# Attention and a PReLU MLP on one core: score tiles in bursts of three, small inputs as rows, and a later second load

## The chip, the cores and the metric

The kernel runs on one core of a Trainium2 chip. Five engines work side by side, each through its own queue in order: TensorE (PE; its weight loads are shown as PEld), VectorE (DVE), ScalarE (ACT), GpSimd (POOL) and SyncE (SP), which only issues DMAs here. ACT and POOL issue DMAs too. The metric is the device time of one execution in microseconds (us), lower is better.

## The reference

Per head, q and k are normalised by their root mean square over the 64 elements of a head and scaled by g_q and g_k; then comes softmax attention, and a two-layer MLP with a parametric ReLU over all heads of a token. The shapes are 8 batches, 12 heads, 448 positions, head size 64, so 768 model columns, and 2048 MLP columns. In and out are float32.

```python
def rmsnorm(x, g):
    rms = np.sqrt(np.mean(x * x, axis=-1, keepdims=True) + 1e-06)
    return x / rms * g
q_n, k_n = (rmsnorm(q, g_q), rmsnorm(k, g_k))
scores = np.matmul(q_n, k_n.transpose(0, 1, 3, 2)) / np.sqrt(64)
attn = np.exp(scores - np.max(scores, axis=-1, keepdims=True))
attn = attn / (np.sum(attn, axis=-1, keepdims=True) + 1e-09)
x = np.matmul(attn, v).transpose(0, 2, 1, 3).reshape(3584, 768)
h = x @ w_in
out = (np.maximum(h, 0.0) + alpha * np.minimum(h, 0.0)) @ w_out
```

## The kernel before

The 96 heads are worked in 24 groups of four: a group y has batch y // 3. Everything is laid out by hand; a tile framework adds the semaphores, and the order on each engine is the order in which the program is written (`manual_schedule`).

**One group.** `load_qk` (L88) brings q and k, two DMAs each, by SP; of groups 0 and 1 ACT issues one half. `square` (L120) and `reduce` (L130) give the sums of squares: the square is on ACT for groups 0 and 1, on POOL later; the reduction is on VectorE. `root` (L138) is two activations on ACT, Ln and Exp. `scale` (L147) multiplies q or k by it and writes float16, on POOL (on VectorE for three early ones). `turn` (L157) transposes both with 14 TensorE matmuls into the PSUM tile tps, and VectorE copies it to qT and kT; kT is multiplied by the product of the gains on the way.

A group has seven score tiles. `score` (L184) makes one with four matmuls of shape 64*64, `soft` (L198) takes its exponential on ACT from PSUM to expT. There are two PSUM buffers for score tiles (pool pss). When the seven tiles are done, `den` (L221) sums them with 28 matmuls against ones (dn), `log` (L225) and `invert` (L230) turn the sum into its reciprocal by Ln and Exp on ACT, and `attv` (L234) multiplies expT with v in 28 matmuls (av); VectorE writes the product with the reciprocal to xT. The PSUM tiles tps, dn and av share one buffer (pool psa).

**The MLP of a batch.** `up` (L245) is one of 16 units: six matmuls (hT, shape 128*128), then ah = alpha * h on ACT, then gT = max(h, ah) on VectorE, in float16. `down` (L262) is one of 14 units for two batches: 16 matmuls (op), a copy to osb on VectorE, and after the second half two output DMAs on SP. Both use the two PSUM buffers of pool psf. Down units of a pair of batches are possible when their columns of gT are there.

**The order.** The 168 score tiles go two at a time; such a pair with what follows it is called a burst here (L413 to L457), 86 in all. The last two bursts hold no tiles. In a burst stand, in this order: the two score tiles; dn, if a group's last tile was in the burst before (`dens`); av one burst later (`avs`); the exponentials; log; roots; a turn, if one is due (`turns`); then the ups and downs that were dealt to this burst (`gaps`), and inversion after the second up or after all units. In bursts with neither dn, av nor turn whose first unit is an up, the second exponential is put behind that up (`wait`). The dealing (L348 to L370) spreads a batch's units over the bursts of the next batch's attention by estimated costs (`cost`, UP, DOWN). Units that are left are in `rest` and come after all bursts. Bursts before `first` have no units and get idle matmuls (`spin`, L284) instead, which keep TensorE running.

Loads and squares are placed by burst as well (`prep`, `post`, `jobs`, L306 to L326): group y's load eight bursts, its squares two bursts ahead of its reduction; reductions in `jobs` are issued inside the first down of the burst, ahead of its copy, or else at the burst's end. POOL's queue holds, besides squares and scalings, the DMAs of v, w_in and w_out.

**The start.** Group 0's loads, the table load on ACT (L381), the gains by POOL, one element per partition (L382 to L384), groups 1 and 2, and alpha by SP, transposed by the access pattern into 128 partitions (L387). Then come 34 idle matmuls on TensorE, the squares, roots, scalings and turn of group 0, and v and w_in on POOL.

Of the kernel before, what the change touches and what calls it, by code (L numbers as in the profile page):

```python
# [9 lines left out]
FP32 = mybir.dt.float32  # L10
# [11 lines left out]
def kernel(  # L22
# [12 lines left out]
    nc = tc.nc  # L35

    B, H, S, D = q.shape
    DM = H * D
    DF = moe_w_in.shape[1]
    J = S // 64  # L40
# [34 lines left out]
    idle = cst.tile([128, S], FP16, name="idle", tag="idle")  # L75
    nc.vector.memset(idle, 0.0)
    gain = cst.tile([128, 1], FP32, name="gain", tag="gain")
    gk2 = cst.tile([128, 1], FP32, name="gk2", tag="gk2")
    alpha_sb = cst.tile([128, NF], FP32, name="alpha_sb", tag="alpha_sb")
    w_in_sb = cst.tile([128, KM, DF], FP16, name="w_in_sb", tag="w_in_sb")  # L80
# [6 lines left out]

    def load_qk(y):  # L88
        b, i = divmod(y, G)
        for nm in "qk":  # L90
            t = ld.tile([128, 2, J, D], FP32, name="nat", tag="nat", bufs=6)
            for g in range(2):
                (nc.scalar if y < 2 and g else nc.sync).dma_start(
                    out=t[ds(64 * g, 64)].rearrange("p h j d -> p h (j d)"),
                    in_=SRC[nm][b, g, :, ds(2 * i, 2)],
                )
            nat[y, nm] = t
# [197 lines left out]

    NB = (NG * J + 1) // 2

    def last(y):
        return (J * y + J - 1) // 2

    dens = {last(y) + 1: y for y in range(NG)}
    avs = {last(y) + 2: y for y in range(NG)}
    prep, post, roots = {}, {}, {}
# [6 lines left out]

    turn_at = [J * y // 2 - 1 for y in range(NG)]
    turns = {n: y for y, n in enumerate(turn_at) if y}
    jobs = {}
    for y in range(G, NG):

        n = turn_at[y - 1] if y < G + 2 else last(y - G) + 2
        at(n - 8, load_qk, y)
        for nm in "qk":
            at(n - 2, square, y, nm)
            if y < G + 2:  # L320
                after(n, reduce, y, nm)
            else:
                jobs.setdefault(n, []).append((reduce, (y, nm)))
        roots[n + 1] = y
    for b in range(1, B):
        at(J * G * b / 2 - 4, load_v, b)  # L326

# [4 lines left out]
    for b in range(B):  # L332
        ups = [(UP, up, (b, ft)) for ft in range(NF)]
        odd = b % 2
        new = [
            (DOWN, down, (b - odd, t, oh))
            for t in (range(3, J) if odd else range(3)) for oh in range(2)
        ]
        tail = len(new) if b == B - 1 else 2 + odd
        periods.append((ups, carry, new[:tail]))  # L340
        carry = new[tail:]

    def cost(n):
        return 0.75 + (1.35 if n in dens or n in avs else 0.0) + (0.9 if n in turns else 0.0)

    first = last(G - 1) + 2
    gaps = [[] for _ in range(NB + 2)]
    for b in range(B - 1):  # L348
        lo = last(G * b + G - 1) + 2
        hi = last(G * b + 2 * G - 1) + 2  # L350
        ups, old, new = (list(u) for u in periods[b])
# [3 lines left out]
        for n in range(lo, hi):  # L355
            clock += cost(n)
            free = n in avs or n in turns
            while ups or old or new:
# [9 lines left out]
                ahead = 0.5 * (UP if ups else DOWN)  # L368
                if n < hi - 1 and clock + ahead > per * (n - lo + 1):
                    break  # L370
# [10 lines left out]
    nc.scalar.preload_act_table_set("natural_log_exp_and_others")  # L381
    for g in range(2):  # L382
        nc.gpsimd.dma_start(out=gain[ds(64 * g, 64)], in_=g_q.unsqueeze(1))
        nc.gpsimd.dma_start(out=gk2[ds(64 * g, 64)], in_=g_k.unsqueeze(1))  # L384
    load_qk(1)
    load_qk(2)
    nc.sync.dma_start(out=alpha_sb, in_=moe_alpha.rearrange("(t p) -> p t", p=128))  # L387

# [4 lines left out]
    for nm in "qk":  # L393
        root(0, nm)
        scale(0, nm)
    nc.vector.tensor_mul(out=gain, in0=gain, in1=gk2)
    turn(0)
# [6 lines left out]
    for c in range(4):  # L404
        load_w_in(c)
        at(8 + 2 * c, load_w_out, c)
    after(0, root, 1)
# [4 lines left out]

    for n in range(NB + 2):  # L413
        for f, a in prep.get(n, ()):
            f(*a)
        tiles = [divmod(m, J) for m in (2 * n, 2 * n + 1) if m < NG * J]
        for t in tiles:
            score(*t)
        if n in dens:
            den(dens[n])  # L420
        if n in avs:
            attv(avs[n])

        plain = n not in dens and n not in avs and n not in turns
        wait = plain and gaps[n] and gaps[n][0][0] is up
        late = []
        for t in tiles[:1] if wait else tiles:
            soft(*t)
        if wait:
# [4 lines left out]
        if n in roots:  # L434
            y = roots[n]
            root(y)
            for nm in "qk":
                scale(y, nm)
        if n in turns:
            turn(turns[n])  # L440
        done = 0
        for f, a in gaps[n]:
            if f is down:
                down(*a, jobs.pop(n, ()))
            else:
                f(*a)
                done += 1
                if late and done == late[0][0]:
                    for _, g, c in late:
                        g(*c)  # L450
                    late = []
        for _, g, c in late:
            g(*c)
        if n < first:
            spin(4 if plain else 1)
        for f, a in jobs.pop(n, []) + post.get(n, []):
# [33 lines left out]
```

## Time and profile before

| what | value |
|---|---|
| median of 4 runs | 484.17 us (483.77 to 485.53) |
| profiled execution | 484.10 us, span 482.2 us, mean granted TensorE clock 0.991 |
| TensorE busy, share of the span | 450.5 us, 93% |
| ScalarE busy | 289.1 us, 60% |
| VectorE busy | 217.3 us, 45% |
| POOL busy | 167.0 us, 35% |
| DMA | 45.46 MB in 32187 packets, 5008 of them under 512 bytes |
| first score tile | starts at 16.02 us |
| first up unit | starts at 50.99 us |
| first down unit | starts at 85.14 us |
| issue to landing, median | gains 5.8 and 7.4 us, alpha 7.1 us, w_in 18.5 us, w_out 14.4 us, v 5.5 us |

The span runs from the first to the last instruction; the execution's time is 1.9 us longer. Rows of a timeline read: start, length (both in us), engine, line, operation, output <- inputs, shape, count, and in brackets the idle time of the engine before it with what ended it. Matmuls are pipelined: a row's length holds the last one's way through the array, so the start of the next row tells more than the end of this one. A window's row has its bounds and length, then busy time of PE, PEld, DVE, ACT and POOL, the granted clock, the share of DMA and its rate.

### The profile page before, as it was taken

To read this page: it belongs to the slowest core of one execution; us is meant where nothing else is said; L and a number is where in the kernel's file an instruction comes from. 1 tells how busy PE (TensorE), PEld (TensorE's weight loads), DVE (VectorE), ACT (ScalarE), POOL (GpSimd) and SP (SyncE) were. 2 spreads that over 40 slices of the span, in tenths; PEclk is the share of its full clock that TensorE was granted. 3 is DMA by queue.
4 is the path that set the end of the run, shared out by engine and by line. 5 is a ranking of instruction groups with operands and counts; after the bars stand their busy time and mean duration, and the time that the engine had idled before them with its cause. 6 is when DMAs were issued, how large, how long until landed. Compare 5 with 4: busy or idle time off the path is not lost.

```text
span 482.2 us, 9494 instructions
## 1 busy us (share of the span) xinstructions
PE 450.5 (93%) x4074; PEld 235.2 (49%) x4074; DVE 217.3 (45%) x312; ACT 289.1 (60%) x399; POOL 167.0 (35%) x123
## 2 busy tenths in 40 slices
PE   7677799999999999999999999999999999999995
PEld 3343444545455544554545554554545554555463
DVE  2744554555354455355363354454462443334421
ACT  3788788657756656656864757558675558423300
POOL 3768735553352260441532441522613200000000
PEclk9799999999999999999999999999999999999999
DMA  7999997350805343432704435413401110111122
GB/s 185 191 254 228 240 230 137 78 141 2 168 0 135 86 111 58 110 84 61 162 5 110 110 84 85 110 44 99 92 1 34 35 34 1 34 34 33 34 65 67
DMA packets 32187, 45.46 MB, mean 94 GB/s; under 512 B 5008, under 2 KB 28560, under 8 KB 32144
## 3 DMA queue, kind: packets, MB, share of 16 engines
q1 hardware_dynamic: 19792, 32.13, 25.8%
q0 software_dynamic: 11776, 11.80, 15.7%
q10 hardware_dynamic: 576, 0.92, 0.7%
q8 instruction: 32, 0.52, 0.5%
q14 instruction: 11, 0.09, 0.1%
HBM read 45.62 MB, written 11.01 MB: 117 GB/s over the span
## 4 chain that ended last, share of the span: by engine, by line
PE 69%; ACT 13%; DVE 8%; issue 4%; POOL 3%; DMA 2%; SPq 0%; POOLq 0%; DVEq 0%; ACTq 0%
PE op L266 30%; PE hT L249 19%; ACT ah L257 6%; PE av L212 6%; PE sc L189 6%; PE dn L212 4%; DVE gT L258 4%; ACT expT L201 4%; DVE ss L133 3%; PE tps L166 3%; DMA nat<-in_k_dram 2%; POOL qs L150 1%; POOL sq L127 1%; ACT rden L227 1%; ACT rr L144 1%
## 5 line engine op out<-in xcount | busy, mean ns | idle before, releaser
L201 ACT ACTIVATE expT<-sc,expb 128x896 f16<-128x896 f32 x168 | 160.4, 1004 | 51.6 <-PE sc L189 51.5
L249 PE MATMUL hT<-xT,w_in_sb 128*128 128x448 f16 x768 | 159.9, 352 | 8.1 <-DVE gT L258 6.5
L266 PE MATMUL op<-w_out_sb,gT 128*128 128x384 f16 x896 | 153.3, 326 | 1.7 <-DVE gT L258 1.7
L257 ACT ACTIVATE ah<-hT,alpha_sb 128x448 f16<-128x448 f32 x128 | 80.7, 635 | 97.2 <-PE hT L249 96.2
L258 DVE TENSOR_TENSOR gT<-hT,ah 128x448 f16<-128x448 f32 x128 | 79.5, 625 | 123.5 <-ACT ah L257 123.3
L150 POOL TENSOR_TENSOR qs<-nat,rr 128x896 f16<-128x896 f32 x45 | 75.0, 1688 | 129.1 <-ACT rr L145 105.3
L266 PEld LDWEIGHTS <-gT 128*128 128x128 f16 x896 | 85.2, 98 | 64.3 <-issue 11.2
L249 PEld LDWEIGHTS <-w_in_sb 128*128 128x128 f16 x768 | 72.4, 97 | 86.0 <-issue 26.2
L127 POOL TENSOR_TENSOR sq<-nat 128x896 f32<-128x896 f32 x44 | 73.0, 1678 | 85.8 <-DVE ss L133 85.8
L278 DVE COPY osb<-op 128x384 f32<-128x384 f32 x56 | 31.1, 556 | 86.5 <-PE op L266 86.5
L189 PE MATMUL sc<-qT,kT 64*64 64x448 f16 x672 | 51.4, 367 | 10.4 <-DVE kT L176 4.5
L133 DVE TENSOR_REDUCE ss<-sq 128x14 f32<-128x896 f32 x48 | 49.7, 1076 | 8.3 <-ACT sq L125 8.3
L240 DVE TENSOR_TENSOR xT<-av,rden 128x896 f16<-128x896 f32 x24 | 26.2, 1092 | 29.9 <-PE av L212 29.9
L212 PE MATMUL av<-expT,vt 64*64 64x448 f16 x672 | 36.0, 349 | 1.3 <-ACT rden L227 1.3
L212 PE MATMUL dn<-expT,ones 64*64 64x448 f16 x672 | 35.9, 349 | 0.0
L189 PEld LDWEIGHTS <-kT 64*64 64x64 f16 x672 | 13.9, 105 | 43.2 <-issue 32.6
L166 PE MATMUL tps<-ident,qs 128*128 128x128 f16 x336 | 24.2, 224 | 3.7 <-POOL qs L150 3.3
L212 PEld LDWEIGHTS <-vt 64*64 64x64 f16 x672 | 20.0, 107 | 13.6 <-issue 2.4
L212 PEld LDWEIGHTS <-ones 64*64 64x64 f16 x672 | 19.9, 107 | 11.8 <-issue 0.3
L166 PEld LDWEIGHTS <-qs 128*128 128x128 f16 x336 | 19.4, 99 | 12.4 <-issue 5.6
L227 ACT ACTIVATE rden<-dn 128x896 f32<-128x896 f32 x24 | 22.1, 921 | 3.5 <-PE dn L212 3.5
L232 ACT ACTIVATE rden<-rden 128x896 f32<-128x896 f32 x24 | 22.6, 943 | 0.3
(25 smaller groups left out, 97.4 us busy)
## 6 DMA issues: line engine op xcount, KB each, us to landing
out_dram<-osb SPq DMA_DIRECT2D x56, 192.0 KB, 2.7
nat<-in_q_dram SPq DMA_DIRECT2D x46, 224.0 KB, 3.9
nat<-in_k_dram SPq DMA_DIRECT2D x46, 224.0 KB, 4.8
vt<-in_v_dram POOLq DMA_DIRECT2D x16, 336.0 KB, 5.5
w_in_sb<-in_moe_w_in_dram POOLq DMA_DIRECT2D x4, 768.0 KB, 18.5
w_out_sb<-in_moe_w_out_dram POOLq DMA_DIRECT2D x4, 768.0 KB, 14.4
nat<-in_q_dram ACTq DMA_DIRECT2D x2, 224.0 KB, 5.8
nat<-in_k_dram ACTq DMA_DIRECT2D x2, 224.0 KB, 7.6
```

Of the source, the lines that this page charges most:

```text
L127: nc.gpsimd.tensor_mul(out=sqf, in0=src, in1=src)
L133: nc.vector.tensor_reduce(out=ss_t[y][:, "qk".index(nm)].rearrange("p h j -> p (h j)").unsqueeze(2), in_=sqs[y, nm], axis=AXIS_X, op=ALU.add,)
L150: eng.tensor_mul(out=t.rearrange("p j h d -> p h j d"), in0=nat[y, nm], in1=rr_t[y][:, "qk".index(nm)].unsqueeze(3).broadcast_to((128, 2, ...
L166: nc.tensor.transpose(tp[:, j, :], qs[y, nm][:, j].rearrange("p h d -> p (h d)"), ident)
L189: nc.tensor.matmul(out=sc[ds(64 * g, 64), par, :S], lhsT=kT[ds(64 * par, 64), g, j, :], rhs=qT[ds(64 * par, 64), g].rearrange("p j c -> p ...
L201: nc.scalar.activation(out=expT[y][:, j], in_=scs[y, j][:, :, :S], func=AF.Exp, scale=QK_SCALE, bias=expb[:, 0:1],)
L212: nc.tensor.matmul(out=acc[ds(64 * par, 64), g, :S], lhsT=weights(g, par, j), rhs=e[ds(64 * g, 64), j, par, :], start=(j == 0), stop=(j == ...
L249: nc.tensor.matmul(out=hT[:, :S], lhsT=w_in_sb[:, c, ts(ft, 128)], rhs=x[:, c, :], start=(c == 0), stop=(c == KM - 1),)
L257: nc.scalar.activation(out=ah, in_=hT[:, :S], func=AF.Copy, scale=alpha_sb[:, ft : ft + 1])
L258: nc.vector.tensor_max(out=gT[:, ft, ds((b & 1) * S, S)], in0=hT[:, :S], in1=ah)
L266: nc.tensor.matmul(out=op[:, :OH], lhsT=gT[:, ft, ts(t, 128)], rhs=w_out_sb[:, ft, ds(oh * OH, OH)], start=(ft == 0), stop=(ft == NF - 1),)
L278: nc.vector.tensor_copy(out=o[:, ds(oh * OH, OH)], in_=op[:, :OH])
```

## The change

**Bursts of three.** The bursts are laid out ahead of the loop. A burst with dn or av takes a third tile; one without takes two. There are 63 bursts instead of 86. The first two tiles stand before dn or av with their exponentials, the third tile and its exponential behind it. A burst's turn now comes behind its first unit instead of before all units, and always in a burst without dn. A reduction is always in a dn burst, a load five bursts ahead of it. The dealing lets a waiting down go first in every burst (`free = True`), gives at least two units to a burst with a turn, and holds back other numbers of downs per batch (`tail`). The bursts without units get four idle matmuls each. Only bursts without dn and av hold back the second exponential.

**Rows.** alpha comes as 16 rows of 128 and each gain as a row written twice, by five DMAs on POOL's queue, into a tile of 18 rows. TensorE transposes it once in float32, VectorE copies the columns out of PSUM; alpha is used from there, and the product of the gains is taken from it. A second identity matrix of 32 columns is made for this.

**The hold.** Before the loads of group 1, ACT copies one column into the tile that q of group 1 goes to. ACT takes it after its table load, so the DMAs into that tile wait for it.

```diff
+    ident32 = cst.tile([32, 32], FP32, name="ident32", tag="ident32")
+    make_identity(nc, ident32)
+    rows = cst.tile([NF + 2, 128], FP32, name="rows", tag="rows")
+    cols = cst.tile([128, NF + 2], FP32, name="cols", tag="cols")
+    alpha_sb = cols[:, :NF]
...
-    def load_qk(y):
+    def load_qk(y, hold=False):
...
+            if hold and nm == "q":
+                nc.scalar.copy(out=t[:, 0, 0, 0:1], in_=expb)
...
+    bursts, dens, avs, first_in, last_in = [], {}, {}, {}, {}
+    m = 0
+    while m < NG * J or len(avs) < NG:
+        n = len(bursts)
+        if len(dens) > len(avs):
+            avs[n] = len(avs)
+        elif len(dens) < NG and last_in.get(len(dens), n) < n:
+            dens[n] = len(dens)
+        count = min(3 if n in dens or n in avs else 2, NG * J - m)
+        bursts.append([divmod(m + c, J) for c in range(count)])
...
-    turn_at = [J * y // 2 - 1 for y in range(NG)]
+    turn_at = {
+        y: max(n for n in range(first_in[y]) if n not in dens) for y in range(1, NG)
+    }
...
-        n = turn_at[y - 1] if y < G + 2 else last(y - G) + 2
-        at(n - 8, load_qk, y)
+        n = max(d for d in dens if d <= turn_at[y] - 2)
+        at(n - 5, load_qk, y)
...
-        at(J * G * b / 2 - 4, load_v, b)
+        at(av_at[G * b] - 4, load_v, b)
...
-        tail = len(new) if b == B - 1 else 2 + odd
+        tail = len(new) if b == B - 1 else 2 if odd or b == 0 else 1
...
-            free = n in avs or n in turns
+            free = True
...
+                short = n in turns and len(gaps[n]) < 2
-                if n < hi - 1 and clock + ahead > per * (n - lo + 1):
+                if n < hi - 1 and not short and clock + ahead > per * (n - lo + 1):
...
-    for g in range(2):
-        nc.gpsimd.dma_start(out=gain[ds(64 * g, 64)], in_=g_q.unsqueeze(1))
-        nc.gpsimd.dma_start(out=gk2[ds(64 * g, 64)], in_=g_k.unsqueeze(1))
-    load_qk(1)
+    nc.gpsimd.dma_start(out=rows[:NF], in_=moe_alpha.rearrange("(t p) -> t p", p=128))
+    for n, g in enumerate((g_q, g_k)):
+        for h in range(2):
+            nc.gpsimd.dma_start(
+                out=rows[NF + n : NF + n + 1, ds(64 * h, 64)], in_=g.unsqueeze(0)
+            )
+    load_qk(1, True)
     load_qk(2)
-    nc.sync.dma_start(out=alpha_sb, in_=moe_alpha.rearrange("(t p) -> p t", p=128))
...
-    nc.vector.tensor_mul(out=gain, in0=gain, in1=gk2)
+    ct = psf.tile([128, 512], FP32, name="ct", tag="mm")
+    nc.tensor.transpose(ct[:, : NF + 2], rows, ident32[: NF + 2, : NF + 2])
+    nc.vector.tensor_copy(out=cols, in_=ct[:, : NF + 2])
+    nc.vector.tensor_mul(out=gain, in0=cols[:, NF : NF + 1], in1=cols[:, NF + 1 : NF + 2])
...
-        at(8 + 2 * c, load_w_out, c)
+        at(7 + c, load_w_out, c)
...
-        for t in tiles:
+        for t in tiles[:2]:
             score(*t)
+        plain = n not in dens and n not in avs
+        wait = plain and gaps[n] and gaps[n][0][0] is up
+        for t in tiles[:1] if wait else tiles[:2]:
+            soft(*t)
         if n in dens:
             den(dens[n])
         if n in avs:
             attv(avs[n])
+        for t in tiles[2:]:
+            score(*t)
+            soft(*t)
...
-        if n in turns:
-            turn(turns[n])
...
+            if k == 0 and n in turns:
+                turn(turns[n])
...
-            spin(4 if plain else 1)
+            spin(4)
```

## The prediction

> **What bounds the kernel now.** I read the page's engine rows first, then a table of windows, then the timeline of TensorE in the steady part, then the timeline of the first 17 us. The profiled execution took 484.10 us for a span of 482.2 us (1.9 us around it) and lies 0.07 us under the median, so differences in span are taken as differences in time.
>
> ```profile
> PE 450.5 (93%) x4074; PEld 235.2 (49%) x4074; DVE 217.3 (45%) x312; ACT 289.1 (60%) x399; POOL 167.0 (35%) x123
> PE   7677799999999999999999999999999999999995
> ```
>
> TensorE is the bound from about 50 us on; before that it waits. The windows (start:end, length, then busy time of PE, PEld, DVE, ACT, POOL) say it in numbers, and that one stretch of two batches comes twice in exactly 110.86 us:
>
> ```profile
> 16.00:50.00 34.00, 26.08 (x322) 12.29 (x326) 16.98 (x18) 28.97 (x38) 26.49 (x21) 0.95 1.18 233
> 138.94:249.80 110.86, 107.89 (x1005) 56.61 (x1004) 52.91 (x77) 70.82 (x99) 42.34 (x29) 1.00 0.38 88
> 249.80:360.66 110.86, 107.89 (x1004) 56.61 (x1004) 52.91 (x77) 70.82 (x99) 42.33 (x29) 1.00 0.35 80
> ```
>
> Busy here hides much. The pure lengths come from start to start in streams: a score tile 0.19 (four matmuls), dn or av 1.31 (28), an up unit 1.12 (six hT), a down unit 2.60 (16 op), a turn 0.79 (14 tps). Two batches are 42 tiles, 12 dn or av, 32 ups, 14 downs and 6 turns: 100.6 us. So 10.3 us of each 110.86 are lost. One burst shows the first half of the loss:
>
> ```profile
> 92.86 0.57 PE L189 MATMUL sc<-qT,kT 64*64 64x448 f16 x8
> 93.26 1.49 PE L212 MATMUL av<-expT,vt 64*64 64x448 f16 x28
> 94.69 2.77 PE L266 MATMUL op<-w_out_sb,gT 128*128 128x384 f16 x16
> 97.39 0.57 PE L189 MATMUL sc<-qT,kT 64*64 64x448 f16 x8
> ```
>
> It takes 4.53 from score to score; its parts are 0.37 + 1.31 + 2.60 = 4.28. So going from 64*64 to 128*128 matmuls and back costs 0.25 a burst (0.03 of step from sc to av is not counted again): 21 bursts, 5.3 us, with 0.4 of steps. The other 4.6 us per two batches are stalls.
>
> **The change, part by part.**
>
> *Fewer bursts.* 86 become 63, 15 instead of 21 per two batches. That removes 6 x 0.25 = 1.5 us and adds 0.3 of steps between dn or av and the third tile: -1.2. In 46 dn and av bursts a third tile stands on TensorE behind dn or av and ahead of all ups and downs. There are two sc buffers, so it waits for the exponential of the first tile. This is the wait that the change adds, and the burst's whole MLP work queues behind it.
>
> *When is that exponential done?* Ordinarily it starts 0.64 after its scores, takes 1.0, and ends at 1.64, while TensorE reaches the third tile at 0.37 + 0.03 + 1.31 + 0.03 = 1.74: no cost. But where the dn burst before ended with an up, ScalarE has that up's ah and then the inversion of dn to do first. Before shows such a place:
>
> ```profile
> 112.56 0.14 PEld L189 LDWEIGHTS <-kT 64*64 64x64 f16 x8 [0.37 <-issue]
> 112.67 0.63 ACT L257 ACTIVATE ah<-hT,alpha_sb 128x448 f16<-128x448 f32 x1 [0.44 <-PE hT L249]
> 113.20 0.94 ACT L232 ACTIVATE rden<-rden 128x896 f32<-128x896 f32 x1
> 114.04 1.90 ACT L201 ACTIVATE expT<-sc,expb 128x896 f16<-128x896 f32 x2
> ```
>
> The first exponential starts 1.48 after the scores, so it ends at 2.48, and a third tile could go at 2.52: 0.78 late. In before nothing on TensorE waits for it. In the changed order I find it in eight av bursts (after dn bursts 19, 26, 34, 36, 41, 49, 51, 59, whose unit lists end in an up with the inversion behind it): 6.2 us over the run, 2.3 of them (bursts 27, 35, 37) in two batches. The Trainium skill, TensorEngine Tiling (PSUM Bottleneck), says that tiling speeds up TensorE but not PSUM evacuation; the trace agrees, with the 1.48 us of lag; without it the sum would be lower by the 6.2.
>
> *Dn bursts that begin with two ups.* The third exponential also pushes the log of dn and the first ah back:
>
> ```profile
> 403.95 2.44 PE L249 MATMUL hT<-xT,w_in_sb 128*128 128x448 f16 x12
> 404.54 0.93 ACT L227 ACTIVATE rden<-dn 128x896 f32<-128x896 f32 x1
> 405.34 0.65 ACT L257 ACTIVATE ah<-hT,alpha_sb 128x448 f16<-128x448 f32 x1
> 406.03 0.63 DVE L258 TENSOR_TENSOR gT<-hT,ah 128x448 f16<-128x448 f32 x1 [2.51 <-ACT ah L257]
> 406.70 1.30 PE L249 MATMUL hT<-xT,w_in_sb 128*128 128x448 f16 x6 [0.31 <-DVE gT L258]
> ```
>
> The scores were at 402.12, the third unit at 4.58 after them. One exponential more (0.9) makes it 5.48, where TensorE would be ready at 2.06 + 2.24 = 4.30 (2.06 is the new base of a dn or av burst: 1.74 + 0.19 + 0.13). That is 1.2 us in bursts 11, 14, 21, 31 and 46: 6.0 over the run.
>
> *Reductions without a down.* Where a dn burst has no down (11, 14, 21), the two sums of squares (2.07) go to VectorE after the last gT, 1.4 us into the av burst; the product into xT (1.09) stands behind them and ends at 4.55. The turn after the first up reuses av's PSUM buffer and would come at 3.18: 1.37 late in bursts 12, 15, 22, 4.1 in all. Elsewhere a down covers it (2.60).
>
> *Others.* Three ups in a row cost 0.44 (the row at 427.70: third hT at 2.68 instead of 2.24), five 0.86. A turn with one up behind it: copies of qT and kT end 2.21 after its start, 0.23 late.
>
> *Two batches of the new order* (bursts 24 to 38): 100.6 + 15 x 0.25 + 24 x 0.03 + stalls 2.3 (third tile) + 1.2 (burst 31) + 1.3 (28, 29, 33) + 0.35 (37) + 0.86 (38) + 0.28 (32, 35) = 111.3. Against 110.86: +0.45, and it comes twice: +0.9. What the bursts save goes into the third tile's wait.
>
> *From the first down to the first repeat* (85.14 to 138.64, 53.5 us; bursts 15's down to 23): 2.7 + 4.8 + 6.7 + 5.5 + 7.0 + 7.5 + 6.6 + 7.75 + 5.9 = 54.5, +1.0. *The end* (360.66 on, 121.54): bursts 54 to 62 by the same sums, then 13 downs, 16 ups and five triples, then 5.1 after the last matmul: 121.8, +0.3.
>
> *Start to the first down, before the load changes.* ScalarE and the chain turn, kT, score, exp set the pace. Replayed with rows: exponentials run at 0.9 each from 16.66; turn 2 waits for the first xT (33.1), its tile goes at 35.45 (34.8 before); the squares of group 3 move on POOL ahead of the scaling of group 2, which ends at 31.85 instead of 30.25, still before turn 2; dn of group 2 ends its log at 50.05, first full up at 52.9 (52.31 before, but with two tiles more done). Then the units come in bunches: kT of turn 4 at 56.75 is 1.1 late, burst 11 takes 6.6, 12 7.75, 13 5.9 (0.73 for four ups), 14 6.6, 15 up to its down 5.4: first down at 89.0, +3.9.
>
> Four warm-up matmuls in each burst without units, where dn, av and turn bursts had one (0.56 more), stand before scores that wait for ScalarE or kT by more than that (0.65 at turn 2), so nothing; uncovered, 0.56 in each of five bursts, 2.8.
>
> *The loads.* The second row below is the wait for k's half of the first group:
>
> ```profile
> 5.25 0.95 ACT L125 ACTIVATE sq<-nat 128x896 f32<-128x896 f32 x1 [1.81 <-DMA nat<-in_q_dram]
> 9.62 0.95 ACT L125 ACTIVATE sq<-nat 128x896 f32<-128x896 f32 x1 [3.41 <-DMA nat<-in_k_dram]
> 12.84 1.87 PE L166 MATMUL tps<-ident,qs 128*128 128x128 f16 x14 [2.83 <-POOL qs L150]
> ```
>
> A copy of about 0.2 (as the Exp of 128x14) after the table load (2.16 + 1.28) holds group 1 to 3.65 instead of 2.19. Behind it wait ScalarE's two issues (done by 4.9, before the square at 5.25) and on SP all of groups 1 and 2. Group 0 then has the DMA engines for 1.4 us more. Bounds: 0, if k is slow for itself, to -3.4, the whole wait (the idle warm-up matmuls end at 10.01, and the squares of group 1 start at 12.17 when its data is in). I take -2.5, nearer the row of k. Alpha and the gains: SP loses one issue (0.41) that nothing waited for; POOL gets a second identity (under 0.5) and five issues instead of four, so the rows are issued by 4.8 and landed, at 5.8 to 7.4 us as the gains do, by 10.6 to 12.2. TensorE's transpose of them (0.1 to 0.5, seven 128-wide ones take 0.93) stands ahead of turn 0, which the earlier k would allow at 10.3: inside the 2.5 if rows land by 10.6, up to 1.5 lost otherwise. The copy of 128x18 (near the 0.15 product) is hidden while the transposes run. w_out's first piece now goes before the second v on POOL's queue; v issued near 45 has until the av of burst 12 near 62, against 18 us at the worst for this queue (w_in's median 18.5): 0, or some 2 if it is late.
>
> Sum: +3.9 - 2.5 + 1.0 + 0.9 + 0.3 = +3.6: 484.2 + 3.6 = 487.8.
>
> **The rivals.** (1) *ScalarE is not late* (faster): the exponentials keep up with three tiles a burst, because downs come first in most bursts and empty its queue. Then the third tile's 6.2 us go, and in the five dn bursts with two ups first the 0.7 that the third exponential adds to the 0.5 of before (3.5): 478.1. It decides if the first exponential of an av burst starts under 0.74 us after its scores. For it: after dn bursts 24, 29, 31 the rule is kept; against it: the 1.48 above. The Trainium skill, TensorEngine Tiling (Key Properties), says that a change of tiling mode drains TensorE; the 0.25 per burst agrees with it, and who counts by that rule alone comes to this rival. (2) *The hold gains nothing* (the change doesn't do what it says): k is slow by itself; 490.3. For it: ScalarE's half of k takes 7.6 us to land, with few bytes ahead of it. (3) *Late second v*: 489.8. (4) *Half the stalls*: VectorE and ScalarE take 4 us less of them: 484, no change.
>
> **How the numbers follow.** A measurement of this kernel tells 0.3% (1.5 us) from no change. Forecast 0.44, rival 1 0.28, rival 2 0.12, rival 3 0.04, rival 4 0.12. Slower 0.60, same 0.12, faster 0.28. The forecast's own range is 485.7 to 490.5; over all cases 477.2 (rival 1 with the whole 3.4 of the loads) to 492.3 (rivals 2 and 3 together).
>
> **What would show it.** In the profile after: 63 bursts, TensorE's sc waiting for expT at L208 some eight times 0.8 us; tps waiting for xT three times; hT waiting for gT in bursts with three ups; two batches in 111.3 us; the second square at about 7 instead of 9.62, the first score near 13.5. Wrong, if two batches take under 109 us, or the first score stands at 16 or later.

## The result and the profile after

The changed kernel takes 484.56 us (median; 484.15 to 485.31), the kernel before 484.04 in the same set of runs. The ratio is 1.0009, with an interval of 1.0004 to 1.0014: slower by some 0.5 us, well inside the 0.3% that count as no change. The forecast was 487.8. Its sign was right and its size was not: +3.6 us were predicted, +0.5 came. The profiled execution took 484.55 us for a span of 482.8 us (482.2 before).

The engine rows of the page after hardly differ from those of before:

```profile
PE 449.0 (93%) x4091; PEld 242.5 (50%) x4091; DVE 218.8 (45%) x313; ACT 288.5 (60%) x400; POOL 168.1 (35%) x126
...
PE   8788888999899999999999999999999999999996
```

TensorE is the bound as before, and the first slices are fuller. The table of windows after shows where the time lies (start:end, length, then busy time of PE, PEld, DVE, ACT and POOL, the clock, the share of DMA and its rate):

```profile
16.00:50.00 34.00, 27.99 (x353) 14.04 (x353) 17.99 (x19) 29.88 (x40) 30.35 (x24) 0.99 1.18 245
85.89:140.11 54.22, 51.11 (x495) 27.51 (x492) 26.66 (x38) 35.58 (x49) 26.40 (x19) 1.00 0.46 104
140.11:250.86 110.75, 106.54 (x1005) 58.47 (x1004) 53.14 (x76) 70.44 (x98) 42.50 (x28) 1.00 0.40 92
250.86:361.62 110.76, 106.55 (x1005) 58.48 (x1004) 53.29 (x77) 70.44 (x98) 42.51 (x28) 1.00 0.33 74
361.62:482.80 121.18, 113.37 (x877) 62.53 (x876) 41.83 (x66) 46.30 (x63) 3.33 (x2) 0.99 0.14 37
```

The first down starts at 85.89, burst 24's scores at 140.11, and from there two batches repeat in 110.75 us. In these two batches TensorE is busy 1.35 us less than before (106.54 against 107.89) in a stretch that is only 0.11 shorter. So bursts of three did save TensorE's time, and nearly all of it went into waiting. Stretch by stretch:

| stretch | before | predicted | after |
|---|---|---|---|
| first score | 16.02 | near 13.5 | 13.53 |
| start to first down | 85.14 | 86.5 | 85.89 |
| first down to the repeat | 53.5, as the prediction took it | 54.5 | 54.22 |
| two batches, twice | 110.86 | 111.3 | 110.75 and 110.76 |
| the rest | 121.54, as the prediction took it | 121.8 | 121.18 |

The waits on TensorE that the prediction named are there. Two bursts in TensorE's timeline after show them. Burst 26, a dn burst, is undisturbed (rows: start, length, engine, line, operation, output <- inputs, shape, count):

```profile
155.20 0.57 PE L196 MATMUL sc<-qT,kT 64*64 64x448 f16 x8
155.60 1.49 PE L219 MATMUL dn<-expT,ones 64*64 64x448 f16 x28
156.93 0.36 PE L196 MATMUL sc<-qT,kT 64*64 64x448 f16 x4
157.22 2.77 PE L273 MATMUL op<-w_out_sb,gT 128*128 128x384 f16 x16
```

From the first score to the first down are 2.02 us: 0.40 for two tiles, 1.33 for dn, 0.29 for the third tile and the change of shape. Burst 27, the av burst behind it, in the timeline of TensorE and ScalarE:

```profile
162.19 0.57 PE L196 MATMUL sc<-qT,kT 64*64 64x448 f16 x8
162.30 0.63 ACT L264 ACTIVATE ah<-hT,cols 128x448 f16<-128x448 f32 x1 [0.50 <-PE hT L256]
162.60 1.49 PE L219 MATMUL av<-expT,vt 64*64 64x448 f16 x28
162.83 0.94 ACT L239 ACTIVATE rden<-rden 128x896 f32<-128x896 f32 x1
163.67 2.80 ACT L208 ACTIVATE expT<-sc,expb 128x896 f16<-128x896 f32 x3
164.72 0.38 PE L196 MATMUL sc<-qT,kT 64*64 64x448 f16 x4 [0.63 <-ACT expT L208]
165.04 2.77 PE L273 MATMUL op<-w_out_sb,gT 128*128 128x384 f16 x16
```

ScalarE does the last up's ah and the inversion (L239, 0.94) before the first exponential, which starts 1.48 behind the scores. So the third tile stands 2.53 behind the first score, not 1.73, and the down starts at 2.85 instead of 2.02: 0.83 late. TensorE's idle time in that row is only 0.63, because av's modelled end covers part of the delay. The start of the down tells the price, the bracket does not.

The start after, from the timeline of ScalarE, TensorE and VectorE:

```profile
3.44 0.19 ACT L98 COPY nat<-expb 128x1 f32<-128x1 f32 x1
...
7.49 0.95 ACT L132 ACTIVATE sq<-nat 128x896 f32<-128x896 f32 x1 [1.25 <-DMA nat<-in_k_dram]
...
10.39 0.23 PE L419 MATMUL ct<-ident,rows 18*128 18x18 f32 x1
...
13.53 0.96 PE L196 MATMUL sc<-qT,kT 64*64 64x448 f16 x8 [1.31 <-DVE kT L183]
```

The holding copy takes 0.19, k of group 0 is there at 7.49 instead of 9.62, the transpose of the rows takes 0.23, and the first score comes 2.49 earlier. Of these, 2.13 stand at k's square; the other 0.36 come behind it, and the load experiments below show from where.

### The profile page after: what moved, and what is told of

The parts are those of the page before. It is cut to its first block, busy times and chain, and to the rows that moved or that the text cites. A ratio compares the mean times of both kernels' runs of the same rounds, so it can differ in the third digit from the quotient of the medians.

```text
span 482.8 us, 9544 instructions
## 1 busy us (share of the span) xinstructions
PE 449.0 (93%) x4091; PEld 242.5 (50%) x4091; DVE 218.8 (45%) x313; ACT 288.5 (60%) x400; POOL 168.1 (35%) x126
## 4 chain that ended last, share of the span: by engine, by line
PE 70%; ACT 15%; DVE 9%; issue 3%; DMA 1%; SPq 0%; DVEq 0%; ACTq 0%
PE op L273 31%; PE hT L256 21%; ACT expT L208 7%; PE sc L196 6%; ACT ah L264 5%; PE dn L219 5%; PE tps L173 4%; DVE gT L265 4%; PE av L219 3%; DVE ss L140 2%; ACT rden L239 2%; DMA nat<-in_k_dram 1%; DVE xT L247 1%; DVE kT L183 1%; DVE qT L181 1%
## 5 line engine op out<-in xcount | busy, mean ns | idle before, releaser
L208 ACT ACTIVATE expT<-sc,expb 128x896 f16<-128x896 f32 x168 | 157.5, 1006 | 22.6 <-PE sc L196 22.4
L264 ACT ACTIVATE ah<-hT,cols 128x448 f16<-128x448 f32 x128 | 80.7, 635 | 138.1 <-PE hT L256 137.8
L196 PE MATMUL sc<-qT,kT 64*64 64x448 f16 x672 | 54.1, 365 | 11.2 <-ACT expT L208 7.3
L196 PEld LDWEIGHTS <-kT 64*64 64x64 f16 x672 | 18.6, 105 | 43.8 <-issue 31.9
L173 PE MATMUL tps<-ident,qs 128*128 128x128 f16 x336 | 23.0, 219 | 5.2 <-DVE xT L247 4.4
L173 PEld LDWEIGHTS <-qs 128*128 128x128 f16 x336 | 20.6, 98 | 9.6 <-issue 5.5
L239 ACT ACTIVATE rden<-rden 128x896 f32<-128x896 f32 x24 | 22.8, 950 | 0.2
```

What stands on the lines that cost most here:

```text
L173: nc.tensor.transpose(tp[:, j, :], qs[y, nm][:, j].rearrange("p h d -> p (h d)"), ident)
L196: nc.tensor.matmul(out=sc[ds(64 * g, 64), par, :S], lhsT=kT[ds(64 * par, 64), g, j, :], rhs=qT[ds(64 * par, 64), g].rearrange("p j c -> p ...
L208: nc.scalar.activation(out=expT[y][:, j], in_=scs[y, j][:, :, :S], func=AF.Exp, scale=QK_SCALE, bias=expb[:, 0:1],)
L239: nc.scalar.activation(out=r, in_=r, func=AF.Exp, scale=-1.0)
L264: nc.scalar.activation(out=ah, in_=hT[:, :S], func=AF.Copy, scale=alpha_sb[:, ft : ft + 1])
```

## The experiments

The theory is the prediction's: the hold brings about 2.5 us at the start, and bursts of three cost because of the named waits, each of them due to the order on ScalarE or VectorE. The rivals: the rows, not the hold, bring the gain at the start; or the bursts cost for another reason than these waits (the number of units per burst, the place of the third tile, the dealing), so that taking the waits away would not give the time back.

### The load changes alone, on the kernel before

The hold, the rows, and both, each put on the kernel before. The hold:

```diff
-    def load_qk(y):
+    def load_qk(y, hold=False):
...
+            if hold and nm == "q":
+                nc.scalar.copy(out=t[:, 0, 0, 0:1], in_=expb)
...
-    load_qk(1)
+    load_qk(1, True)
```

> The kernel before with the hold alone; gains and alpha still come one element per partition. Theory (k of group 0 is slow because group 1 shares its transfers): the second square starts near 7.5 and 2.5 us are gained, near 481.5. Rival (the element-wise gains and alpha are what slows the first transfers): under 0.7 us gained, the second square at 9 or later.

The rows, as in the change itself (five DMAs on POOL, the transpose, the copy, alpha's DMA gone from SP):

```diff
-    for g in range(2):
-        nc.gpsimd.dma_start(out=gain[ds(64 * g, 64)], in_=g_q.unsqueeze(1))
-        nc.gpsimd.dma_start(out=gk2[ds(64 * g, 64)], in_=g_k.unsqueeze(1))
+    nc.gpsimd.dma_start(out=rows[:NF], in_=moe_alpha.rearrange("(t p) -> t p", p=128))
+    for n, g in enumerate((g_q, g_k)):
+        for h in range(2):
+            nc.gpsimd.dma_start(
+                out=rows[NF + n : NF + n + 1, ds(64 * h, 64)], in_=g.unsqueeze(0)
+            )
...
-    nc.sync.dma_start(out=alpha_sb, in_=moe_alpha.rearrange("(t p) -> p t", p=128))
...
-    nc.vector.tensor_mul(out=gain, in0=gain, in1=gk2)
+    ct = psf.tile([128, 512], FP32, name="ct", tag="mm")
+    nc.tensor.transpose(ct[:, : NF + 2], rows, ident32[: NF + 2, : NF + 2])
+    nc.vector.tensor_copy(out=cols, in_=ct[:, : NF + 2])
+    nc.vector.tensor_mul(out=gain, in0=cols[:, NF : NF + 1], in1=cols[:, NF + 1 : NF + 2])
```

> The kernel before with the rows alone, no hold. Theory: the second square stays near 9.6, and the time within 0.7 us of before (484). Rival (element-wise packets are the cause): the second square near 7.5 and some 2.5 us gained, near 481.5.

Both of these edits together:

> The kernel before with both load changes (rows and hold), bursts of two kept. Theory: the 2.5 us by which the first score comes earlier (13.53 instead of 16.02) pass through the whole start, since every engine's chain there hangs on the one before: first score near 13.5, first up near 48.5, and 2.5 us less than before, near 481.5. Rival (the start is paced by ScalarE and the transfers, which take the gain back before the first up): first score near 13.5, but the time within 0.7 us of before.

And the gains as rows alone, with a tile of two rows, alpha loaded as before:

```diff
-    for g in range(2):
-        nc.gpsimd.dma_start(out=gain[ds(64 * g, 64)], in_=g_q.unsqueeze(1))
-        nc.gpsimd.dma_start(out=gk2[ds(64 * g, 64)], in_=g_k.unsqueeze(1))
+    for n, g in enumerate((g_q, g_k)):
+        for h in range(2):
+            nc.gpsimd.dma_start(out=rows[n : n + 1, ds(64 * h, 64)], in_=g.unsqueeze(0))
```

> The kernel before with the two gains as rows, alpha still one element per partition. Theory (the gains' 256 packets of 4 bytes are on their way while k of group 0 is; alpha starts at 11.4, after it): second square near 8.4 and first score near 14.8 as with all rows, time near 482.5. Rival (alpha is what the rows gain by): second square near 9.6, time as before.

Measured:

| kernel | median us | ratio to before, interval | second square | first score |
|---|---|---|---|---|
| before | 483.93 | | 9.62 | 16.02 |
| hold | 483.25 | 0.9989 (0.9967 to 1.001) | 8.62 | 15.03 |
| rows | 481.63 | 0.9953 (0.9935 to 0.9972) | 8.36 | 14.77 |
| gains as rows alone (in a set with 484.22 for before) | 482.01 | 0.9957 (0.9943 to 0.9970) | 7.94 | 13.98 |
| rows and hold | 481.05 | 0.9936 (0.9914 to 0.9958) | 7.38 | 13.42 |

The second square, from ScalarE's timeline with the gains as rows alone:

```profile
7.94 0.95 ACT L129 ACTIVATE sq<-nat 128x896 f32<-128x896 f32 x1 [1.79 <-DMA nat<-in_k_dram]
```

The whole gain of 2.9 us stands against the prediction's 2.5, but not by its cause. At k's square the hold alone gives 1.00 us, the rows alone 1.26, and both together 2.24: these two add up, and the rows, which the prediction took as at best free, give the larger part. The gains as rows without alpha give 1.68 there, so alpha's rows, issued ahead of them on the same queue, take 0.42 back. In time the hold alone is not told from before: its interval takes in 1.

Behind k's square, TensorE's granted clock makes a difference of 0.36 us. From the square to the first score the profiled runs take 6.40 or 6.41 us (before, hold, rows) or 6.04 (gains as rows alone, rows and hold, the changed kernel). In the first three the clock stood at half for most of group 0's turn: 0.50 from about 13 to 19 us in before, from 12 to 18 with the hold and with the rows. With rows and hold it was full throughout, and in the changed kernel the turn was over before a half clock from 14 to 16 us. In the changed kernel with the loads of before (below) only the second seven transposes met half a clock (0.93 instead of 0.56 us), and it takes 6.40 too. The turn shows it, first with the hold, then with rows and hold:

```profile
11.85 1.88 PE L168 MATMUL tps<-ident,qs 128*128 128x128 f16 x14 [2.02 <-POOL qs L152]
...
10.60 0.56 PE L172 MATMUL tps<-ident,qs 128*128 128x128 f16 x7 [0.44 <-POOL qs L156]
11.55 0.56 PE L172 MATMUL tps<-ident,qs 128*128 128x128 f16 x7 [0.38 <-DVE qs L156]
```

So the 2.60 of the first score with both is 1.00 of the hold, 1.24 of the rows on top of it and 0.36 of the clock; what sets the clock was not tried.

The DMA engines show that the gain of the rows is not a matter of fewer transfers ahead of k. The DMA view of the first 16 us in 40 slices of 0.4 us (busy tenths, then GB/s), of before:

```profile
DMA  0000056999859653546899999999999999999999
GB/s 0 0 0 0 0 72 152 372 300 233 117 152 197 170 166 99 171 175 198 265 327 354 323 287 269 242 215 229 255 224 229 220 246 186 147 155 115 99 114 83
```

and with the gains as rows:

```profile
DMA  0000028999999998999999999999999999999999
GB/s 0 0 0 0 0 58 228 327 314 264 206 265 220 224 211 215 274 269 265 318 296 287 233 238 211 202 260 229 251 246 233 230 117 137 111 67 101 140 161 141
```

From 4.0 to 7.6 us the DMA engines of before are busy 30 to 90% of the time and move 99 to 198 GB/s; with the gains as rows they stay 80% busy or more, at 206 to 274. The software queue of POOL has 11776 packets in both kernels, so the number of packets does not explain it. The expectation's 256 packets of 4 bytes are not there: both traces list 64 packets of 16 bytes on that queue, which by their bytes are the gains. Why a load of 64 elements into 64 partitions leaves the other queues short of work is not settled here. One small rival is untried: with the rows, POOL makes the second identity matrix first and issues the gains 0.20 us later (1.66 instead of 1.46).

### The bursts of three alone

The changed kernel with the rows and the hold undone:

```diff
-    load_qk(1, True)
+    for g in range(2):
+        nc.gpsimd.dma_start(out=gain[ds(64 * g, 64)], in_=g_q.unsqueeze(1))
+        nc.gpsimd.dma_start(out=gk2[ds(64 * g, 64)], in_=g_k.unsqueeze(1))
+    load_qk(1)
     load_qk(2)
+    nc.sync.dma_start(out=alpha_sb, in_=moe_alpha.rearrange("(t p) -> p t", p=128))
...
+    nc.vector.tensor_mul(out=gain, in0=gain, in1=gk2)
```

> The changed kernel with the loads of before: gains and alpha one element per partition, no hold. Theory (loads and bursts act in different stretches and add): 484.6 + 2.9 = 487.5, the first score near 16.0. Rival (the bursts of three are paced by ScalarE in the start and would take the loads' gain away): 484.6 to 485.5.

Measured: 487.37 us, 1.0065 (1.0048 to 1.0082). The first score is at 15.99, the first down at 88.34. So the bursts of three cost 3.2 us by themselves (487.37 against 484.22 in the same set; 3.5 when the changed kernel is set against the load changes alone, 484.56 against 481.05), and the load changes give 2.8 with bursts of three, 2.9 without. The prediction had +6.1 for the bursts. The two halves of the change nearly cancel.

Two tiles per burst in the new order, with all else of the changed kernel:

```diff
-        count = min(3 if n in dens or n in avs else 2, NG * J - m)
+        count = min(2, NG * J - m)
```

> The changed kernel with two tiles in every burst: 86 bursts again, all else (loads, downs first, turn behind the first unit, reductions in dn bursts) kept. Theory (a burst costs 0.27 in shape changes, the third tile's waits cost 6.5 us, the later log in five dn bursts 2.5): 484.6 + 21 x 0.27 - 6.5 - 2.5 = 481.3. Rival (the third tile's waits cost nothing in the end, the bursts saved are the whole effect of the tiling): 484.6 + 5.7 = 490.3. Second rival: the dealing itself, made for bursts of three, leaves longer runs of ups: over 484.

Measured: 493.79 us, 1.0199 (1.0175 to 1.0222). The theory (481.3) and the first rival (490.3) did not have that. The second rival's bound of 484 takes it in, but longer runs of ups are not what the waits show. The list of waits of this kernel (engine and line, what was waited for: us in total, times, longest):

```profile
PEld L173 <- POOL qs L157: 11.2, 11, 2.1
...
PE tps L173 <- POOL qs L157: 9.0, 11, 1.8
...
PE av L219 <- DMA vt<-in_v_dram: 3.3, 2, 2.5
```

A turn waits eleven times for POOL's scaling, up to 2.1 us, which the changed kernel hardly does (the same row there has 0.2 us for the weight load). The new rules place turns and reductions by the dn bursts; that with 86 bursts this leaves POOL too little time ahead of a turn is an inference from that row, not tried by itself. And v of batch 1 comes late: its DMAs stand behind all four of w_out on POOL's queue here (issued at 46.83, landed by 67.44), and av waits for them in burst 15. That burst takes 10.93 us, against 4.20 for the same work in before; behind the wait TensorE's clock was at half (0.50 from 67 to 73 us). So what the prediction's rival 3 feared happened here. This run doesn't isolate the number of tiles per burst. Its two batches in the steady part (254.85 to 366.38) take 111.53 us, 0.78 more than with three tiles, with some of the turns' waits among them.

### The wait for the third tile

The inversion goes directly behind the log where the dn burst's first unit is a down, so that it isn't left between the last up's ah and the next exponential:

```diff
         if n in dens:
             log(dens[n])
-            late = [(2, invert, (dens[n],))]
+            if gaps[n] and gaps[n][0][0] is down:
+                invert(dens[n])
+            else:
+                late = [(2, invert, (dens[n],))]
```

> The changed kernel, where a dn burst whose first unit is a down puts the inversion directly behind the log, not behind the ups. Theory (the third tile of the next av burst waits for its buffer, because ScalarE has an ah and the inversion before the exponential): the eight waits of 0.8 us between av and the third tile go, the units behind them keep their lengths, two batches take 108.3 instead of 110.75, the time is 484.6 - 6.5 = 478.1. Rival (ScalarE is simply behind, so the exponential is late either way, or the gain turns into waits for gT or kT in the same bursts): less than 2 us gained.

Measured: 477.85 us, 0.9870 (0.9832 to 0.9908); two batches take 108.26. Burst 27 in the timeline of TensorE and ScalarE:

```profile
161.20 0.57 PE L196 MATMUL sc<-qT,kT 64*64 64x448 f16 x8
161.30 0.63 ACT L264 ACTIVATE ah<-hT,cols 128x448 f16<-128x448 f32 x1 [0.50 <-PE hT L256]
161.84 2.80 ACT L208 ACTIVATE expT<-sc,expb 128x896 f16<-128x896 f32 x3
162.92 0.36 PE L196 MATMUL sc<-qT,kT 64*64 64x448 f16 x4
163.22 2.77 PE L273 MATMUL op<-w_out_sb,gT 128*128 128x384 f16 x16
```

The exponential starts 0.64 behind the scores instead of 1.48, and the third tile waits for nothing. Burst 27 is 7.77 long instead of 8.60, bursts 20 and 35 6.88 instead of 7.71, 37 6.36 instead of 7.20. Eight bursts by 0.83 are 6.6; the median fell by 6.7. The cause named for this term is shown, and its size (6.2 predicted) was nearly right. The Trainium skill, TensorEngine Tiling (Array Packing), section PSUM Bottleneck, says that tiling speeds TensorE and not the emptying of PSUM. This run agrees, with a qualification: ScalarE is busy 60% of the span, and what lacked was not its throughput but its order; an activation of 0.94 us moved earlier in eight places is worth 1.4%.

### The reductions in bursts of ups alone

Sums of squares go to VectorE ahead of the ups where a dn burst has no down, so that the product into xT isn't queued behind them:

```diff
         done = 0
+        if gaps[n] and all(f is up for f, _ in gaps[n]):
+            for f, a in jobs.pop(n, []):
+                f(*a)
         for k, (f, a) in enumerate(gaps[n]):
```

> The changed kernel, where a dn burst without downs (11, 14, 21, and the ones of ups alone) issues the two reductions ahead of its ups, not behind them. Theory (in bursts 12, 15 and 22 the turn waits for xT, which stands behind those reductions on VectorE): the three waits of 1.3 us go, and nothing else moves, 484.6 - 3.9 = 480.7. Rival (the reductions then delay gT of the ups in the dn burst, so that the third up comes later by as much): within 1 us of the changed kernel.

The wait in the changed kernel, burst 12 (VectorE and TensorE):

```profile
61.86 2.07 DVE L140 TENSOR_REDUCE ss<-sq 128x14 f32<-128x896 f32 x2
62.56 1.31 PE L256 MATMUL hT<-xT,w_in_sb 128*128 128x448 f16 x6
63.85 1.08 DVE L247 TENSOR_TENSOR xT<-av,rden 128x896 f16<-128x896 f32 x1
64.98 0.94 PE L173 MATMUL tps<-ident,qs 128*128 128x128 f16 x14 [1.11 <-DVE xT L247]
```

and the same burst with the edit:

```profile
62.27 1.09 DVE L247 TENSOR_TENSOR xT<-av,rden 128x896 f16<-128x896 f32 x1 [0.55 <-PE av L219]
62.34 1.31 PE L256 MATMUL hT<-xT,w_in_sb 128*128 128x448 f16 x6
63.48 0.94 PE L173 MATMUL tps<-ident,qs 128*128 128x128 f16 x14
```

Measured: 480.91 us, 0.9934 (0.9915 to 0.9952). The turn stands 1.14 behind the up's start instead of 2.42. Bursts 12 and 22 fall from 7.58 to 6.36, 15 from 7.91 to 6.64: 3.7 in all, and the median fell by 3.65 (4.1 predicted).

### The third unit behind two ups, and all three edits together

What is left of the named waits is the third up of dn bursts 11, 14, 21, 31 and 46. In the timeline of burst 11 after, it waits 0.82 for gT, because the third exponential stands ahead of log and ah on ScalarE:

```profile
55.38 1.90 ACT L208 ACTIVATE expT<-sc,expb 128x896 f16<-128x896 f32 x2
...
56.05 2.44 PE L256 MATMUL hT<-xT,w_in_sb 128*128 128x448 f16 x12
57.16 0.93 ACT L234 ACTIVATE rden<-dn 128x896 f32<-128x896 f32 x1
57.95 1.21 ACT L264 ACTIVATE ah<-hT,cols 128x448 f16<-128x448 f32 x2
...
59.32 1.29 PE L256 MATMUL hT<-xT,w_in_sb 128*128 128x448 f16 x6 [0.82 <-DVE gT L265]
```

On top of the two edits above, the third exponential goes behind the first ah in dn bursts that begin with two ups:

```diff
+        two_ups = n in dens and [g[0] for g in gaps[n][:2]] == [up, up]
         for t in tiles[2:]:
             score(*t)
-            soft(*t)
+            if not two_ups:
+                soft(*t)
...
+                if two_ups:
+                    late = [(1, soft, t) for t in tiles[2:]]
...
                     late = []
+                    if two_ups and done == 1:
+                        late = [(2, invert, (dens[n],))]
```

> The changed kernel with the inversion directly behind the log where the burst's first unit is a down, the reductions ahead of the ups where the burst has no down, and, in dn bursts that begin with two ups, the third tile's exponential behind the first ah. Theory: the three causes add: 6.5 + 3.9 + 5 x 0.55 = 13.1 us less, 471.4. Rival (they overlap, since the same few engines are late in each): over 475.

Measured: 471.12 us, 0.9733 (0.9712 to 0.9754). Bursts 11, 14 and 21 fall from 6.51, 6.71 and 6.51 to 5.93, and 31 and 46 from 8.17 to 7.40: 3.5 in all. The av bursts 12, 15 and 22 behind them take 0.1 more each than with the second edit alone (6.47 for 6.36, 6.74 for 6.64), so some 3.2 are left. This kernel leaves out the inversion of the last group, whose dn burst has no tiles, so its time lacks that work. It is put back in the next one, which excludes bursts without a third tile:

```diff
-        two_ups = n in dens and [g[0] for g in gaps[n][:2]] == [up, up]
+        two_ups = n in dens and len(tiles) > 2 and [g[0] for g in gaps[n][:2]] == [up, up]
```

> The combination of a_best with the one inversion put back that a_best left out (that of the last group, whose dn burst has no tiles). Theory: that inversion runs while TensorE has ups, so the time stays at 471.1 and beats before by 2.6% (ratio 0.973). Rival (a_best was short by the missing work): 472 or more.

Measured: 470.86 us (470.73 to 470.95), 0.9725 (0.9709 to 0.9742) of before: 13.4 us less than before and 13.7 less than the changed kernel. The inversion put back adds no time. Its two batches in the table of windows:

```profile
133.76:241.25 107.49, 105.96 (x1005) 58.48 (x1004) 53.13 (x76) 70.99 (x98) 42.53 (x28) 1.00 0.40 94
```

By the lengths of the bursts the three edits give 6.6, 3.7 and 3.2, 13.5 together: they add up, since they act nearly all in different bursts. The third was not run by itself. So in the changed kernel 13.7 us lay behind three choices of order on ScalarE and VectorE. None of the three was tried on the kernel before, so what they would give with bursts of two is open. The first has less to give there: in before TensorE's score tiles wait 3.0 us in all for exponentials, in the changed kernel 7.3.

### What the third tile's place is worth

In the kernel of 470.86 us the third tile with its exponential goes behind the burst's first unit, where the burst has units. The work is the same, but a burst changes shape twice more; the late exponential behind two ups falls away with it:

```diff
-        for t in tiles[2:]:
+        behind = tiles[2:] if gaps[n] else []
+        for t in tiles[2:] if not behind else []:
             score(*t)
-            if not two_ups:
-                soft(*t)
+            soft(*t)
...
+            if k == 0:
+                for t in behind:
+                    score(*t)
+                    soft(*t)
             if k == 0 and n in turns:
                 turn(turns[n])
```

> The combination, with the third tile of a burst behind the burst's first unit instead of directly behind dn or av. Nothing waits for a buffer then, but 41 bursts with units have one pair of shape changes more. Theory (a pair costs 0.25, less 0.03 of step): 41 x 0.22 to 0.27 = 9 to 11 us more than the combination, 480 to 482. Rival (the 0.25 a burst is something else than the change of shape, such as the first weights of a new group): under 3 us more.

Measured: 478.39 us, 0.9880 (0.9860 to 0.9900): 7.5 us more than with the tile in front. Burst 24 in TensorE's timeline:

```profile
135.38 0.57 PE L196 MATMUL sc<-qT,kT 64*64 64x448 f16 x8
135.78 1.49 PE L219 MATMUL dn<-expT,ones 64*64 64x448 f16 x28
137.21 2.77 PE L273 MATMUL op<-w_out_sb,gT 128*128 128x384 f16 x16
139.91 0.38 PE L196 MATMUL sc<-qT,kT 64*64 64x448 f16 x4
140.23 2.77 PE L273 MATMUL op<-w_out_sb,gT 128*128 128x384 f16 x16
```

It is 7.55 long instead of 7.32, and bursts 25 and 26, 8.00 and 7.22, are also 0.23 longer than 7.77 and 6.99. So a pair of shape changes costs 0.23 where nothing else is in the way, less the small step from dn to the third tile that falls away; that is close to the 0.25 that was read from one burst of before. Bursts that begin with two ups got 0.1 to 0.2 shorter, those of av with ups alone 0.1 to 0.2 longer, one (17) longer by 1.3. The expected 9 to 11 us were too much by 1.5 to 3.5. This is the cost of which the change spares six in two batches. The Trainium skill, TensorEngine Tiling (Array Packing), section Key Properties, says that a change of tiling mode drains TensorE; the runs agree, at 0.23 us for a pair of changes.

## Why the prediction was nearly right in its reasons and too high in its number

The mechanism held: two batches took 110.75 us, not under 109, the first score stood at 13.53, not at 16, and the waits were where they were named. What failed is the sizing of the bursts' terms: +6.1 by the prediction, +3.2 by the medians. Set against before by the spans of the profiled executions, the changed kernel with the loads of before has +3.2 up to the first down, +0.42 to the repeat, -0.22 in the repeats and +0.05 at the end, where the prediction had +3.9, +1.0, +0.9 and +0.3.

- **The loads (-2.5): right in size, wrong in cause.** The first score moved by 2.49, and k's square stands at 7.49 (about 7 was forecast). The prediction gave all of it to the hold and took the rows as at best free. At k's square the hold gives 1.0 us, with or without the rows, and the rows 1.2 to 1.3; the last 0.36 are the clock in the first turn, which no term had. That these sum to the forecast is luck. The rival that the hold gains nothing is refuted at k's square, but by less than the sum supposed. It had leaned on 7.6 us for ScalarE's half of k; that is the median of groups 0 and 1, and for group 0 the trace has 6.27, with SP's half landing last, at 9.53. The rows' smaller steps held: the transpose took 0.23 (0.1 to 0.5 forecast; the 0.93 for seven transposes, from which that was taken, stood at half clock and is 0.56 at full), the holding copy 0.19 (0.2).
- **The third tile's wait (6.2): right.** All eight bursts have it, 0.82 to 0.84 each instead of 0.78. Rival 1, in which ScalarE isn't late, is refuted in the kernel as changed. Its condition, the first exponential under 0.74 behind the scores, is met in those bursts only once the inversion is moved (0.64), and then the time falls by 6.7, where the rival had 6.2 for it.
- **Reductions without a down (4.1) and two ups first (6.0).** The first measured 3.7. Of the second, the one edit tried gave back 3.5 in the five bursts; the prediction's own split was 2.5 that before already had and 3.5 that the third exponential adds, so this agrees with what the change added. The burst lengths came out as named: 6.51, 7.58, 5.84 and 6.71 for bursts 11 to 14 (6.6, 7.75, 5.9 and 6.6 forecast), and 4.72, 6.64, 5.53, 6.99, 7.71, 6.51, 7.58 and 5.84 for 16 to 23 (4.8, 6.7, 5.5, 7.0, 7.5, 6.6, 7.75 and 5.9).
- **The step that failed first: the base of 2.06 for a dn or av burst.** It measured 2.02 (burst 26). Two tiles with their step took 0.40 as forecast, dn with its step 1.33 instead of 1.34, and the third tile with its half of the shape changes 0.29 instead of 0.32. Of the 46 dn and av bursts, 36 lie behind the first down, where TensorE sets the pace: 1.4 us at most. In two batches it is 12 x 0.04 = 0.48 of the 0.55 by which 111.3 was too long (the parts as they stand add up to 111.4). The 0.35 at burst 37 did not occur (the third up is on time there and in burst 52), and slightly longer waits (0.83 for 0.78 and the like) took the remaining 0.28 back. So the +0.45 forecast for two batches came out at -0.11.
- **The end (+0.3), and a slip of bounds.** The first stretch of before was counted to 138.64, the repeats from 138.94, so 0.30 of before stood in no term; to 138.94 that stretch is 53.80. By its own working the sum was +3.3. The end came out at 121.18, 0.6 less than the 121.8 forecast; 0.45 of that lies behind the last output's landing (below) and is no work of the kernel. With the loads of before the end takes 121.59.
- **Start to the first down (+3.9 before the loads): too much by 0.7.** The changed kernel without the load changes has its first down at 88.34, 3.2 later than before, where 89.0 was forecast. Of the 0.7, some 0.3 stand ahead of burst 11 (56.48 instead of 56.75) and 0.4 in bursts 11 to 15.
- Together: 0.3 of bounds, 0.65 at the start, 0.3 to the repeat, 1.1 in the repeats and 0.6 at the end, some 3.0 in all, which is the +3.6 against the +0.6 of the spans. Each was small against its stretch (at most 0.8%), but the sum was a small difference of large terms, and the errors had the same sign.
- **Rival 4 (half the stalls, 484) gave the nearest time, for a wrong reason**: no class of stall was missing. Rival 3 did not occur: v of batch 1 was issued at 45.4 and nothing waited for it. With two tiles in every burst it did, and that burst lost 6.7 us, half a clock included, where some 2 had been allowed.

## What to carry to other kernels

Where a change makes TensorE wait for ScalarE to empty a PSUM buffer, walk ScalarE's queue ahead of that activation. One that nobody is waiting for yet (here the inversion, 0.94 us) cost TensorE nearly its whole length (0.83), and moving it was worth more than the change itself. When a change saves and adds time in the same bursts, take the burst's length from start to start in one place and don't add rounded parts, because 0.04 us in each of 36 bursts is 1.4 us, against an error of 3.0. And before giving up a change that brings nothing, list the waits it adds: here three small edits of order turned +0.1% into -2.75%.

## What was not expected of the hardware

- Four tiny loads, 64 elements into 64 partitions each, held up the big loads of other queues. With the gains as rows and nothing else, k of group 0 was there 1.68 us earlier (square at 7.94 instead of 9.62), and the DMA engines moved 206 to 274 GB/s instead of 99 to 198 in the stretch from 4.0 to 7.6 us, with the same number of packets. The mechanism is open.
- From the last output's landing to the end of the span, the four kernels with alpha's DMA on SP (before, hold, gains as rows, changed without load changes) take 1.35 to 1.36 us, and five without it (rows, rows and hold, changed, inversion moved, the fastest) take 0.91 to 0.92. No run here tells why; 0.45 us of the difference between kernels lies there.
- TensorE's granted clock fell to half near the start in some profiled runs: 0.50 from about 13 to 19 us in before, 14 to 16 us in the changed kernel, not at all with rows and hold. It cost 0.36 us where it met the first turn. From the first score to the fifth burst before takes 9.39 us with it, rows and hold 9.39 without it, and the hold alone 9.73 with it.
- A pair of changes between 64*64 and 128*128 matmuls costs 0.23 us on TensorE, the same in dn and av bursts that begin with a down.
